# A two-layer SSM and MLP block, forward and backward: the main part taken chunk by chunk through both layers

## The chip, the cores and the metric

One core of a Trainium2 chip runs the kernel, in one launch. The time is device microseconds from the start to the end of an execution. PE is the matrix engine (its weight loads are listed apart, as PEld); DVE, ACT and POOL are the vector, scalar and GpSimd engines; SP issues DMAs only. PE sums into PSUM, which ACT and DVE empty; everything else lies in SBUF or, between distant stages, in device memory (names ending in `_d`).

## The reference

S = 2048 tokens, D = 448, F = 1792, one batch, bf16 outside and float32 in sums. `_A_ref` shifts k by a short convolution, multiplies by v, convolves with a long kernel by FFT and multiplies by q, which here is the normalised x; `_B_ref` is an MLP. Two layers use the same weights:

```python
def _B_ref(x, w1, w2):
    h = jnp.einsum("bsd,df->bsf", x, w1)
    h = _silu(h)
    return jnp.einsum("bsf,fd->bsd", h, w2)

x = A_q
x = x + _A_ref(_layernorm(x), A_k, A_v, A_shift_k, A_ssm_k, A_ssm_D)
x = x + _B_ref(_layernorm(x), B_w1, B_w2)
x = x + _A_ref(_layernorm(x), A_k, A_v, A_shift_k, A_ssm_k, A_ssm_D)
x = x + _B_ref(_layernorm(x), B_w1, B_w2)
```

Wanted are x and, for a given grad_out, the gradients of all eight inputs (A_q, A_k, A_v, A_shift_k, A_ssm_k, A_ssm_D, w1, w2). The convolution's result y is the same in both layers, since it doesn't depend on x: it is computed once, and its gradient is the sum of both layers' (`gY`).

## The kernel before

It has three parts. The **prefix** (0 to 109 us of the profile) computes y (`Ysb`) by FFTs as matmuls, stores the spectra, and normalises the first 512 tokens. The **main part** (`Main.run`, from 109.2 us) does the MLPs. The **suffix** (`_ssm_suffix`, first matmul at 563.6 us) takes the FFT back for the gradients of k, v, the kernels and D, and the rest of the weight gradients.

In the main part the tokens are four *chunks* of 512, each of four tiles of 128 tokens. X (float32, all 2048 tokens, in SBUF) holds the residual stream and later its gradient. For a chunk c and a layer L there are four products, each of 56 matmuls with 128x128 weights:

- **h** (L545): w1 by the transposed normalised x (`nT`), 14 blocks of F in banks of two (1024 columns of PSUM, two banks in turn). ACT takes silu from the bank (L549, `aT`), then DVE, or ACT once in a half, copies the same bank out (L551, `dT`), from which ACT later forms silu's slope (L532).
- **out** (L570): aT by w2, one tile of tokens per bank, added to X on DVE (L571). In layer 1, ACT copies X to bf16 and POOL stores it (L575, L577).
- **g** (L599): w2 transposed by the transposed gradient (`gT`); ACT copies (L603), DVE multiplies by the slope (L608, `ghT`).
- **n** (L640): ghT by w1 transposed; ACT scales (L642), DVE does the layer norm's backward (`ln_bwd`, four operations) and writes X; then the product with the first normalised x (`gyt`) and a second layer-norm backward, of the A half (L652).

The order is: layer 0 forward for chunks 0 to 3, layer 1 forward and backward for each chunk, layer 0 backward for chunks 0 to 3. Slopes' inputs, normalised rows and `gyt` of one layer are thus written to device memory and loaded again (`DT_d`, `N_d`, `GY_d`, in `load_l0`). The first half of the next h is issued before out of the present chunk. A scheduler fixes each engine's order by dependences and by estimated costs (`bal` shares copies between ACT and DVE); `high_priority` moves a step ahead.

The weight gradients sum over all 2048 tokens: per 128 of the 1792 rows ("ft"), 16 matmuls (L769) of `dstat` (activations with tokens on the partitions) by a tensor of rows. For them aT and ghT of each half chunk go to device memory: of layer 1 *turned*, by a transposing DMA on SP (L478) into one of two `turned` buffers and a store on POOL (L479); of layer 0 plain (L482), and then the load is a transposing DMA (L741). The w2 gradient is two sums: layer 0's from `mov2`, 10 fts beside layer 0 backward and 4 in the suffix, goes to `W2P_d` in float32 (L779) and is loaded and added later (L790, L795). The last thing is w1's gradient, 14 fts of 32 matmuls, each turned by PE and stored (L800 to L806).

In the suffix, L208 is the first FFT stage (its matrix `M1s` is loaded at L826), L228 and L229 the second inverse one, L879 and L880 its products, L916 the gradient of the long kernel (gK), L959 and L965 the gradient of k: DVE makes four products and PE sums them by matmuls with the identity.

Of the kernel before, what the change touches and what calls it, by code (L numbers as in the profile page):

```python
# [10 lines left out]
FP32 = mybir.dt.float32  # L11
# [6 lines left out]
P = 128  # L18
S = 2048
# [101 lines left out]
def kernel(  # L121
# [35 lines left out]
    k.N_d = [dram.tile([S, D], BF16, name=f"N_d{i}") for i in range(4)]  # L157
    k.DT_d = dram.tile([4, 2, P, NF // 2, 512], BF16, name="DT_d")
    k.A_d = [dram.tile([NF, P, S], BF16, name="A_d0"), dram.tile([P, NF, NT, P], BF16, name="A_d1")]
    k.GH_d = [dram.tile([NF, P, S], BF16, name="GH_d0"), dram.tile([P, NF, NT, P], BF16, name="GH_d1")]  # L160
    k.GY_d = dram.tile([S, D], BF16, name="GY_d")
    k.W2P_d = dram.tile([F, D], FP32, name="W2P_d")
# [18 lines left out]
    k.wk = ctx.enter_context(tc.tile_pool(name="wk", bufs=1))  # L181
    k.dp = ctx.enter_context(tc.tile_pool(name="dp", bufs=1))
    with tc.tile_pool(name="yk", bufs=1, side="right") as yk:
        k.Ysb = yk.tile([P, J, D], BF16, name="Ysb")
        _ssm_prefix(k)
        k.w1sb = k.wk.tile([DC, ND, F], BF16, name="w1sb", tag="WA")
        nc.sync.dma_start(out=k.w1sb[:], in_=k.B_w1.rearrange("(c p) f -> p c f", p=DC))
        k.w2sb = k.wk.tile([P, NF, D], BF16, name="w2sb", tag="WB")
        nc.sync.dma_start(out=k.w2sb[:], in_=k.B_w2.rearrange("(c p) d -> p c d", p=P))
        k.psum = ctx.enter_context(tc.tile_pool(name="psum", bufs=1, space=PSUM, reuse_waits="tile"))  # L190
        k.bal.reset()
        with ExitStack() as es:
            m = Main(k, es)
            m.run()
            with tc.issue_after(k.d0_load.ins):
                _wgrad_w2_first(k, m.td, range(10))
    _ssm_suffix(k)


# [36 lines left out]

def _swap_halves_dma(k, dst, src, lo, hi, eng, dlo=None):
    if dlo is None:
        dlo = lo
    dhi = dlo + (hi - lo)  # L240
    eng.dma_start(out=dst[0:64, dlo:dhi], in_=src[64:128, lo:hi])
    return eng.dma_start(out=dst[64:128, dlo:dhi], in_=src[0:64, lo:hi])
# [6 lines left out]
def _ln(k, pool, c, src, si, n_g, groups=((0, 4),), pin=False, eng=None):  # L249
    nc = k.nc  # L250
    for lo, hi in groups:
# [14 lines left out]
        k.bal.add("dve", 0.8 * n + 0.2)  # L266
        for tl in range(lo, hi):
            e = eng or k.bal.pick(D, act_ns=1.04, dve_ns=0.55, act_fixed=0.28)
            if e is nc.scalar:
                nc.scalar.activation(n_g[:, tl, :], src(tl), ACT.Identity, bias=nmr[:, tl:tl + 1], scale=r[:, tl:tl + 1])  # L270
            else:
                nc.vector.tensor_scalar(out=n_g[:, tl, :], in0=src(tl), scalar1=r[:, tl:tl + 1], scalar2=nmr[:, tl:tl + 1], op0=ALU.mult, op1=ALU.add)
    nc.gpsimd.dma_start(out=_pm(k.N_d[si][:])[:, 4 * c:4 * c + 4, :], in_=n_g[:])


def _ssm_prefix(k):
# [4 lines left out]
    with ExitStack() as es:  # L281
# [6 lines left out]
        k.M1sb = k.wk.tile([P, 16, 2, P], BF16, name="M1sb", tag="WA")  # L288
# [9 lines left out]
        ksb += [k.dp.tile([DC, S], BF16, name="K_sb", tag="dstat", bufs=2)[:] for i in range(2)]  # L298
# [116 lines left out]
        k.x0c0 = k.dp.tile([P, 4, D], BF16, name="x0c0", tag="dstat", bufs=2)  # L415
        nc.gpsimd.dma_start(out=k.x0c0[:], in_=_pm(k.A_q[0])[:, 0:4, :])
        k.na0 = k.dp.tile([P, 4, D], BF16, name="na0", tag="dstat", bufs=2)
# [40 lines left out]

class Main:

    def __init__(self, k, es):
# [3 lines left out]
        self.wt = pool("mwt")  # L465
        self.w2T = self.wt.tile([P, ND, F], BF16, name="w2T")
        self.w1T = self.wt.tile([P, NF, D], BF16, name="w1T")
        self.td = pool("mtd")
        self.ch = pool("mch")
        self.xp = pool("mx", side="right")  # L470
        self.X = self.xp.tile([P, NT, D], FP32, name="X")
        self.w1sb, self.w2sb, self.Y = k.w1sb, k.w2sb, k.Ysb

    def store_turned(self, dst, tile_, c, hh):
        nc = self.nc
        an = self.td.tile([P, NF // 2, 4, P], BF16, name="turned", tag="S", bufs=2)
        for lo, hi in ((0, 4), (4, 7)):
            nc.sync.dma_start_transpose(out=an[:, lo:hi].rearrange("p a t f -> p (a t) f"), in_=tile_[:, lo:hi, :].rearrange("p a s -> p (a s)"))  # L478
        nc.gpsimd.dma_start(out=dst[:, 7 * hh:7 * hh + 7, 4 * c:4 * c + 4, :], in_=an[:])  # L479

    def store_plain(self, dst, tile_, c, hh):
        self.nc.gpsimd.dma_start(out=dst[7 * hh:7 * hh + 7, :, 512 * c:512 * (c + 1)].rearrange("ft f s -> f ft s"), in_=tile_[:])  # L482

    def load_weights_T(self, which):
        nc, k = self.nc, self.k
        if which == 1:
            nc.sync.dma_start_transpose(out=self.w1T[:], in_=k.B_w1)
            return
        nc.sync.dma_start_transpose(out=self.w2T[:, 0:3, :], in_=k.B_w2[:, 0:384])
        nc.sync.dma_start_transpose(out=self.w2T[:, 3:4, :], in_=k.B_w2[:, 320:448])  # L490
        nc.gpsimd.memset(self.w2T[0:64, 3, :], 0.0)

    def transp(self, src, dst, blocks):
        nc, k = self.nc, self.k
        rows = max(hi - lo for lo, hi in blocks)
        for h in range(2):
            pt = k.psum.tile([P, 2, 512], BF16, name="ps_t", tag="tr", bufs=2)
            for u in range(2):
                lo, hi = blocks[2 * h + u]
                for tl in range(4):  # L500
                    nc.tensor.transpose(pt[:rows, u, tl * P:(tl + 1) * P], src[:, tl, lo:hi], k.ident[:])
            _copy(nc, k.bal.pick(1024, dve_ns=0.53), dst[:rows, 2 * h:2 * h + 2, :], pt[:rows])

    def a_fwd(self, c, si, xc, n_g=None, groups=((0, 4),)):
        nc, k, X = self.nc, self.k, self.X
        if n_g is None:
            n_g = self.ch.tile([P, 4, D], BF16, name="na", tag="na", bufs=2)
            src = (lambda tl: xc[:, tl, :]) if xc is not None else (lambda tl: X[:, 4 * c + tl, :])
            _ln(k, self.ch, c, src, si, n_g)
        t1 = self.ch.tile([P, 4, D], BF16, name="a_t1", tag="a_t1")  # L510
        for lo, hi in groups:
            sl = slice(4 * c + lo, 4 * c + hi)
            nc.vector.tensor_tensor(out=t1[:, lo:hi, :], in0=n_g[:, lo:hi, :], in1=self.Y[:, sl, :], op=ALU.mult)
            nc.vector.tensor_tensor(out=X[:, sl, :], in0=xc[:, lo:hi, :] if xc is not None else X[:, sl, :], in1=t1[:, lo:hi, :], op=ALU.add)
        k.bal.add("dve", 3.1)
        return n_g

    def b_pre(self, c, si, groups=((0, 4),), eng=None):
        X = self.X
        n_g = self.ch.tile([P, 4, D], BF16, name="nb", tag="nb", bufs=2)  # L520
        _ln(self.k, self.ch, c, lambda tl: X[:, 4 * c + tl, :], si, n_g, groups, eng=eng)
        return n_g

    def b_tr(self, n_g):
        nT = self.ch.tile([P, ND, 512], BF16, name="nT", tag="nT", bufs=2)
        self.transp(n_g, nT, [(DC * i, DC * i + DC) for i in range(4)])
        return nT

    def slope(self, d):
        for o in range(0, 7, 2):  # L530
            n = min(2, 7 - o)
            self.nc.scalar.activation(d[:, o:o + n, :], d[:, o:o + n, :], ACT.Derivative_silu)  # L532
        self.k.bal.add("act", 3.4)

    def h(self, c, L, nT, half, hold):
        nc, k = self.nc, self.k
        aT = self.td.tile([P, NF // 2, 512], BF16, name="aT", tag="T", bufs=3)
        dT = self.td.tile([P, NF // 2, 512], BF16, name="dT", tag="D", bufs=3)
        hold.append((aT, dT))
        for ft0, n in ((0, 2), (2, 2), (4, 2), (6, 1)) if half == 0 else ((7, 1), (8, 2), (10, 2), (12, 2)):  # L540
            ps = k.psum.tile([P, 2, 512], FP32, name="ps_h", tag="mm", bufs=2)
            for u in range(n):
                ft = ft0 + u
                for dc in range(ND):
                    nc.tensor.matmul(ps[:, u, :], lhsT=self.w1sb[:, dc, ft * P:(ft + 1) * P], rhs=nT[:DC, dc, :], start=(dc == 0), stop=(dc == ND - 1))  # L545
            o = ft0 - 7 * half
            a = aT[:, o:o + n, :]
            tm = dT[:, o:o + n, :]
            nc.scalar.activation(a, ps[:, 0:n, :], ACT.Silu)  # L549
            e = nc.scalar if o == 4 else nc.vector  # L550
            _copy(nc, e, tm, ps[:, 0:n, :])  # L551
            k.bal.add("act", 0.52 * n)
            k.bal.add(*(("act", 0.52 * n) if e is nc.scalar else ("dve", 0.6 * n)))
        if L == 1:
            if half == 1:
                for _, d in hold:
                    self.slope(d)
        else:
            nc.gpsimd.dma_start(out=k.DT_d[c, half], in_=dT[:])
            self.store_plain(k.A_d[0], aT, c, half)  # L560
        if L == 1:
            self.store_turned(k.A_d[1], aT, c, half)

    def out(self, c, aT, last):
# [435 lines left out]
```

## Time and profile before

| | |
|---|---|
| median of 3 timed runs | 848.54 us (840.52 to 859.15) |
| span of the profiled execution | 867.0 us |
| mean clock granted to PE in it | 0.950 |
| instructions | 12590 |
| PE, DVE, ACT busy | 753.6, 527.9, 478.0 us |
| DMA: packets, data | 168391, 178.59 MB |
| prefix, main part, suffix | 0–109.2, 109.2–563.6, 563.6–867.0 us |

The span runs from the first to the last instruction of one execution, taken by the profiler; the timed runs are others. PE's ends are modelled, so its busy time is an upper reading. The page's groups give busy time, mean duration, and the idle time just before an instruction with what ended it: idle time of an engine that nobody waits for costs nothing. The costliest groups of PE, and the DMA that most rows below refer to (issue to landing):

```profile
L599 PE MATMUL ps_g<-gT,w2T 128*128 128x512 bf16 x431 | 104.7, 388 | 17.3 <-ACT ghp L603 16.3
L545 PE MATMUL ps_h<-nT,w1sb 112*128 112x512 bf16 x448 | 106.5, 385 | 3.1 <-ACT nT L111 1.9
...
L113 DVE CAST dT<-ps_h 128x1024 bf16<-128x1024 f32 (+1 forms) x56 | 59.2, 1065 | 31.7 <-ACT aT L549 31.6
```
```profile
A_d<-turned POOLq DMA_DIRECT2D x8, 896.0 KB, 4.7
GH_d<-turned POOLq DMA_DIRECT2D x8, 896.0 KB, 7.3
dTl<-DT_d SPq DMA_DIRECT2D x8, 896.0 KB, 6.0
...
dstat<-A_d SPq DMA_DIRECT2D x14, 512.0 KB, 6.6
dstat<-GH_d SPq DMA_DIRECT2D x14, 512.0 KB, 3.8
```

### The profile page before, as it was taken

The numbers are of one execution on the slowest core, as the hardware profiler recorded it, in microseconds if no ns is written. First come the engines' busy times: TensorE is split into PE (matmuls) and PEld (weight loads), VectorE is DVE, ScalarE is ACT, GpSimd is POOL, SyncE is SP. The second block draws the span as 40 slices with busy tenths as digits, with TensorE's granted clock in tenths as the row PEclk, the third lists the DMA queues.
The fourth block names the chain that finished last, engine by engine and source line by source line (L and its number), as shares of the span: only waits on it lengthen the run. The fifth ranks groups of instructions, "written<-read, shape, count | busy, mean of one in ns | idle before, by whom it ended". The sixth has DMA issues, their size and how long they took to land.

```text
span 867.0 us, 12590 instructions
## 1 busy us (share of the span) xinstructions
PE 753.6 (87%) x4894; PEld 411.7 (47%) x4924; DVE 527.9 (61%) x1060; ACT 478.0 (55%) x573; POOL 143.0 (16%) x218
## 2 busy tenths in 40 slices
PE   6998699999999999999779899950579996999997
PEld 4975344444444444444334344520346664545553
DVE  5789668777349788682779899730156631760100
ACT  5789566669879798998566552230136532330010
POOL 1143223221100211101001011110101121221010
PEclk9999789999999999999899999985789998999999
DMA  9279896656586677899774656999988879987771
GB/s 333 91 244 283 301 248 239 230 211 170 142 173 157 188 196 196 197 210 247 181 251 153 187 170 164 266 177 137 186 260 300 284 258 254 130 236 175 185 186 44
DMA packets 168391, 178.59 MB, mean 206 GB/s; under 512 B 135374, under 2 KB 139086, under 8 KB 167308
## 3 DMA queue, kind: packets, MB, share of 16 engines
q1 hardware_dynamic: 144304, 81.70, 42.0%
q0 software_dynamic: 21696, 88.07, 31.7%
q10 hardware_dynamic: 2332, 8.03, 3.1%
q8 instruction: 38, 0.62, 0.3%
q14 instruction: 21, 0.17, 0.1%
HBM read 66.64 MB, written 70.65 MB: 158 GB/s over the span
## 4 chain that ended last, share of the span: by engine, by line
DVE 18%; DMA 18%; issue 17%; PE 16%; ACT 10%; POOL 2%; POOLq 0%; ACTq 0%; SPq 0%; DVEq 0%
DMA dstat<-A_d 6%; PE ps_d L769 6%; PE ps_o L570 3%; DVE dT L113 3%; DVE lb_u L624 2%; DVE X L625 2%; DMA dTl<-DT_d 2%; ACT ghp L603 2%; DVE lb_junk L621 2%; PE ps_h L545 2%; DMA out_dram<-gKD 2%; PE ps_n L640 2%; DVE ghT L608 2%; DMA dmov<-in_grad_out_dram 2%; DMA xsw_c<-Zg 1%
## 5 line engine op out<-in xcount | busy, mean ns | idle before, releaser
L769 PEld LDWEIGHTS <-dstat 128*128 128x128 bf16 x896 | 87.7, 99 | 122.5 <-DMA dstat<-A_d 39.9
L769 PE MATMUL ps_d<-mov,dstat 128*128 128x448 bf16 x448 | 96.1, 358 | 39.0 <-DMA dstat<-A_d 39.0
L599 PE MATMUL ps_g<-gT,w2T 128*128 128x512 bf16 x431 | 104.7, 388 | 17.3 <-ACT ghp L603 16.3
L545 PE MATMUL ps_h<-nT,w1sb 112*128 112x512 bf16 x448 | 106.5, 385 | 3.1 <-ACT nT L111 1.9
L769 PE MATMUL ps_d<-dmov,dstat 128*128 128x448 bf16 x448 | 97.1, 360 | 4.6 <-DMA dmov<-N_d 2.2
L640 PE MATMUL ps_n<-w1T,ghT 128*128 128x448 bf16 x448 | 93.4, 360 | 4.6 <-ACT lb_u L642 3.5
L570 PE MATMUL ps_o<-w2sb,aT 128*128 128x448 bf16 x448 | 91.5, 353 | 0.8 <-ACT aT L549 0.3
L113 DVE CAST dT<-ps_h 128x1024 bf16<-128x1024 f32 (+1 forms) x56 | 59.2, 1065 | 31.7 <-ACT aT L549 31.6
L599 PEld LDWEIGHTS <-w2T 128*128 128x128 bf16 x448 | 44.4, 99 | 71.6 <-issue 24.9
L603 ACT CAST ghp<-ps_g 128x1024 bf16<-128x1024 f32 x56 | 56.6, 1010 | 34.8 <-PE ps_g L599 12.7
L549 ACT ACTIVATE aT<-ps_h 128x1024 bf16<-128x1024 f32 (+1 forms) x64 | 58.1, 917 | 27.1 <-PE ps_h L545 15.9
L545 PEld LDWEIGHTS <-w1sb 112*128 112x128 bf16 x448 | 44.1, 99 | 57.7 <-issue 12.7
L640 PEld LDWEIGHTS <-ghT 128*128 128x128 bf16 x448 | 43.6, 99 | 49.8 <-issue 9.4
L570 PEld LDWEIGHTS <-aT 128*128 128x128 bf16 x448 | 42.9, 98 | 43.7 <-ACT aT L549 3.8
L800 DVE CAST dout<-ps_d 128x448 bf16<-128x448 f32 x14 | 8.7, 624 | 75.6 <-PE ps_d L769 75.6
L805 ACT COPY do<-ps_dt 112x512 bf16<-112x512 bf16 x14 | 8.2, 586 | 75.1 <-PE ps_dt L803 75.1
L228 PE MATMUL ps_v<-Gsb,pa 128*128 128x128 bf16 x336 | 43.5, 221 | 6.5 <-DVE pa L437 4.1
L229 PE MATMUL ps_v<-Gsb,pb 128*128 128x128 bf16 x336 | 42.0, 222 | 3.1 <-DVE pb L438 1.5
L532 ACT ACTIVATE dTl<-dTl 128x1024 bf16<-128x1024 bf16 (+1 forms) x32 | 28.7, 947 | 18.2 <-DMA dTl<-DT_d 18.2
L608 DVE TENSOR_TENSOR ghT<-dT,ghp 128x1024 bf16<-128x1024 bf16 (+1 forms) x32 | 19.6, 622 | 31.0 <-ACT ghp L603 31.0
L229 PEld LDWEIGHTS <-pb 128*128 128x128 bf16 x336 | 32.7, 99 | 11.9 <-DVE pb L438 5.2
L113 DVE COPY Zg<-ps_tr 128x2048 bf16<-128x2048 bf16 x5 | 6.0, 1222 | 51.0 <-DMA W2P_d<-dpo 47.4
(182 smaller groups left out, 1300.1 us busy)
## 6 DMA issues: line engine op xcount, KB each, us to landing
A_d<-aT POOLq DMA_DIRECT2D x8, 896.0 KB, 5.0
DT_d<-dT POOLq DMA_DIRECT2D x8, 896.0 KB, 6.3
A_d<-turned POOLq DMA_DIRECT2D x8, 896.0 KB, 4.7
GH_d<-turned POOLq DMA_DIRECT2D x8, 896.0 KB, 7.3
dTl<-DT_d SPq DMA_DIRECT2D x8, 896.0 KB, 6.0
GH_d<-ghT POOLq DMA_DIRECT2D x8, 896.0 KB, 8.4
dstat<-A_d SPq DMA_DIRECT2D x14, 512.0 KB, 6.6
dstat<-GH_d SPq DMA_DIRECT2D x14, 512.0 KB, 3.8
```

What stands on the lines that cost most here:

```text
L113: eng.tensor_copy(out, in_)
L228: nc.tensor.matmul(pv[:, i, :], lhsT=pa[:, i * P:(i + 1) * P], rhs=k.Gsb[:, ga, :], start=True, stop=False)
L229: nc.tensor.matmul(pv[:, i, :], lhsT=pb[:, i * P:(i + 1) * P], rhs=k.Gsb[:, gb, :], start=False, stop=True)
L532: self.nc.scalar.activation(d[:, o:o + n, :], d[:, o:o + n, :], ACT.Derivative_silu)
L545: nc.tensor.matmul(ps[:, u, :], lhsT=self.w1sb[:, dc, ft * P:(ft + 1) * P], rhs=nT[:DC, dc, :], start=(dc == 0), stop=(dc == ND - 1))
L549: nc.scalar.activation(a, ps[:, 0:n, :], ACT.Silu)
L570: nc.tensor.matmul(po[:, :D], lhsT=aT[ft // 7][0][:, ft % 7, tl * P:(tl + 1) * P], rhs=self.w2sb[:, ft, :], start=(ft == 0), stop=(ft == N ...
L599: nc.tensor.matmul(ps[:, u, :], lhsT=self.w2T[:, b, ft * P:(ft + 1) * P], rhs=gT[:, b, :], start=(b == 0), stop=(b == ND - 1))
L603: nc.scalar.copy(gh[:], ps[:])
L608: nc.vector.tensor_tensor(out=ghT[hh][:, o:o + len(u), :], in0=dT[hh][1][:, o:o + len(u), :], in1=gh[:, u[0]:u[0] + len(u), :], op=ALU.mult)
L640: nc.tensor.matmul(pn[:, :D], lhsT=ghT[ft // 7][:, ft % 7, tl * P:(tl + 1) * P], rhs=self.w1T[:, ft, :], start=(ft == 0), stop=(ft == NF - 1))
L769: nc.tensor.matmul(ps[:, :D], lhsT=st[:, t, :], rhs=movs[gi][:, t, :], start=(gi == 0 and t == 0), stop=(gi == len(groups) - 1 and t == NT ...
```

## The change

The main part goes chunk by chunk: a chunk's layer 1 backward is followed at once by its layer 0 backward, and the next chunk's forward is laid between. PE's order in the main part and the suffix is the order of the program text (`manual_schedule`), no longer the scheduler's; the other engines are still scheduled.

```diff
+    with tc.manual_schedule(engines={nc.tensor.engine}):
         with ExitStack() as es:
-            m = Main(k, es)
-            m.run()
-            with tc.issue_after(k.d0_load.ins):
-                _wgrad_w2_first(k, m.td, range(10))
-    _ssm_suffix(k)
+            Main(k, es).run()
+        _ssm_suffix(k)
```

Per chunk (jobs are steps of four matmuls of the weight gradients):

```diff
+            gh = self.G(gT, hook=mid_g)
+            aT, dT = self.H(c, 1, nT, range(7))
+            self.slope(dT)
+            if c < 3:
+                self.fwd0(c + 1)
+            self.O(c, 1, aT)
+            self.scale(gh, dT)
+            for hh in range(2):
+                self.store(("g", 1), gh[hh], c, hh)
...
+            self.N(c, 1, gh, lambda tl: gb[:, tl, :], self.n1[1], self.n1[0], hook=mid_n)
...
+            if c < 3:
+                aT, dT1 = self.H(c + 1, 0, nT, (1, 4), hook=mid_h)
+                gb = gb_load(c + 1)
+            else:
+                jobs.start()
+                jobs.run(14)
...
+            gh = self.G(gT, dT0)
...
+                self.slope(dT0)
+                self.O(c + 1, 0, aT, hook=None)
+                self.fwd1(c + 1)
...
+            self.N(c, 0, gh, lambda tl: self.X[:, 4 * c + tl, :], self.n0[c][1], self.n0[c][0], hook=mid_n1)
```

So g of layer 1 comes before h of that layer and is scaled by the slope afterwards (`scale`). X is bf16. `DT_d`, `GY_d` and `W2P_d` are gone; `Y_d` and `G1_d` (y, and the gradient after the layer 0 MLP) are new. aT of both layers is stored turned, in quarter chunks (the two `turned` buffers hold four blocks each):

```diff
-        an = self.td.tile([P, NF // 2, 4, P], BF16, name="turned", tag="S", bufs=2)
         for lo, hi in ((0, 4), (4, 7)):
+            an = self.t([P, 4, 4, P], "turned", "S", 2)
...
+            nc.gpsimd.dma_start(out=dst[:, 7 * hh + lo:7 * hh + hi, 4 * c:4 * c + 4, :], in_=an[:, 0:hi - lo])
```

In layer 1 the output is stored from X itself, which the following n overwrites; the layer norm's backward has five operations:

```diff
-            ob = self.ch.tile([P, 4, D], BF16, name="ob", tag="a_t1")
-            nc.scalar.copy(ob[:], X[:, 4 * c:4 * c + 4, :])
-            nc.gpsimd.dma_start(out=_pm(k.outs[0][0])[:, 4 * c:4 * c + 4, :], in_=ob[:])
+        if L == 1:
+            nc.gpsimd.dma_start(out=_pm(k.outs[0][0])[:, 4 * c:4 * c + 4, :], in_=X[:, 4 * c:4 * c + 4, :])
...
+    nc.vector.scalar_tensor_tensor(out=v[:], in0=u0, scalar=-1.0 / D, in1=n_t, op0=ALU.mult, op1=ALU.mult, accum_out=cp[:, 1:2])
+    nc.vector.tensor_scalar(out=cc[:], in0=cp[:, 0:1], scalar1=-1.0 / D, scalar2=None, op0=ALU.mult)
+    nc.vector.tensor_scalar(out=v[:], in0=n_t, scalar1=cp[:, 1:2], scalar2=cc[:], op0=ALU.mult, op1=ALU.add)
+    nc.vector.tensor_tensor(out=v[:], in0=v[:], in1=u0, op=ALU.add)
+    nc.vector.tensor_tensor(out=G_out, in0=v[:], in1=g_res, op=ALU.add)
```

Normalising is done on DVE alone. In h, silu and the copy alternate per bank (in layer 1 all copies on DVE, in layer 0 those of two banks). All four weight layouts are loaded after the prefix, in the pool `mwt`. The matrix M1s is loaded to space that `mwt` had.

Each ft of w2's gradient is one sum of 32 matmuls (grad_out by a of layer 1, then X, which holds the gradient between the layers, by a of layer 0), and those of w1 as before; all are `Jobs`, of which 24 steps run in the last chunk, and one or two after each step of the suffix, the rest at its end:

```diff
+        keys = (("a", 1), ("a", 0))
+        yield from self.pair((0, 1), keys, (go, g2), self.fin_w2, 12)
...
+        keys = (("g", 1), ("g", 0))
+        yield from self.pair((0, 1), keys, (mov3, mov1), self.fin_w1, NT)
```

In the suffix, swapped halves of the spectrum are DVE copies, no longer DMAs; k's gradient is summed on DVE (64 products of 128x448 and 48 additions for 32 products of 128x896 and 64 matmuls); and the layer-norm backward of the first A half, with its 16 tiles, is done there after loads of `G1_d`, `N_d` and `Y_d`:

```diff
+            for j in range(4):
+                nc.vector.tensor_tensor(out=prods[j], in0=gks[:, g + j, :], in1=skb[:, j, :], op=ALU.mult)
+            for j in range(2):
+                nc.vector.tensor_tensor(out=s_[j][:], in0=prods[2 * j], in1=prods[2 * j + 1], op=ALU.add)
...
+            nc.vector.tensor_tensor(out=gk[:, g % 2, :], in0=s_[0][:], in1=s_[1][:], op=ALU.add)
...
+            nc.vector.scalar_tensor_tensor(out=u1, in0=G1, scalar=k.rstd[0][:, t:t + 1], in1=y, op0=ALU.mult, op1=ALU.mult, accum_out=cp[:, t % 4, 0:1])
+            _ln_bwd(k, p2, u1, n0, cp[:, t % 4, :], G1, G1)
```

## The prediction

> **What bounds the kernel now.** I read the page's busy shares first, by engine and in 40 slices of 21.7 us, with the clock that PE was granted.
>
> ```profile
> ## 1 busy us (share of the span) xinstructions
> PE 753.6 (87%) x4894; PEld 411.7 (47%) x4924; DVE 527.9 (61%) x1060; ACT 478.0 (55%) x573; POOL 143.0 (16%) x218
> ## 2 busy tenths in 40 slices
> PE   6998699999999999999779899950579996999997
> PEld 4975344444444444444334344520346664545553
> DVE  5789668777349788682779899730156631760100
> ACT  5789566669879798998566552230136532330010
> ...
> PEclk9999789999999999999899999985789998999999
> ```
>
> PE is the bound nearly everywhere. It falls at the start, in slices 20 and 21 (layer 0 backward), and to 5, 0 and 5 in slices 27 to 29. What stops it is in the table of waits (waiting engine, tile and line; what it waits for; us in all, times, longest), then in the timeline of SP (start, duration):
>
> ```profile
> POOL GH_d L479 <- DMA turned<-ghT: 67.6, 8, 11.2
> ...
> PE ps_d L769 <- DMA dstat<-A_d: 39.0, 2, 38.3
> ...
> ACT dTl L532 <- DMA dTl<-DT_d: 18.2, 6, 6.7
> ...
> PE ps_g L599 <- ACT ghp L603: 16.3, 9, 5.6
> ```
> ```profile
> 560.73 53.73 SPq L741 DMA_TRANSPOSE dstat<-A_d  x3
> ```
>
> One wait of 38.3 us on PE is for transposing loads of A_d[0], which hold SP's queue for 53.7 us. The busy time by windows (length, then busy us of PE, weight loads, DVE, ACT and POOL, then PE's clock, the DMA share, GB/s) shows the hole, and the thinner stretch of layer 0 backward, where slopes come back from DT_d:
>
> ```profile
> 440.00:460.00 20.00, 15.11 (x67) 7.00 (x68) 14.22 (x33) 11.47 (x17) 0.23 (x1) 0.91 0.45 161
> ...
> 480.00:500.00 20.00, 15.29 (x77) 7.26 (x78) 15.52 (x36) 13.42 (x19) 0.93 (x1) 0.91 0.51 157
> ...
> 580.00:600.00 20.00, 0.00 (x0) 0.00 (x0) 0.00 (x0) 0.00 (x0) 0.00 (x0) 0.50 1.00 125
> 600.00:620.00 20.00, 5.13 (x15) 2.14 (x16) 0.00 (x0) 0.91 (x1) 1.07 (x2) 0.51 1.14 106
> ```
>
> The profiled span is 867.0 us, 18.5 above the median of 848.5 and above the slowest timed run (859.2). I take the hole to be what varies (some 20 us in a median run). The change removes it, so the sum against the profile needs no further shift to be a median.
>
> **The change, part by part.** *PE's work.* A 512-column matmul follows the one before by 0.213 us, one of 448 columns by 0.188, one of 128 by 0.055. Each of h, g, out and n has 56 matmuls per chunk and layer: 11.9 us for h or g (512 columns), 10.5 for out or n (448). Over both layers that is 4 × 11.9 + 4 × 10.5 = 89.8, and 64 transposes of 0.055 add 3.6: 93.4 us per chunk, 373.5 for four, before and after. Before, the main part lasts from 109.2 to 563.6; less 160 matmuls of L769 (30 us) that is 424, so 51 us were waits and slow clock. Moved: 24 steps of four L788 matmuls (18 us) now stand in the last chunk, so the suffix gets 64 more of them than before (+12), and loses 64 gk matmuls of L965 (−12).
>
> *Removed.* The 38.3 us hole and the slow clock after it (660 − 615 = 45 us at 0.87: about 4): −42. A_d[0] is now stored turned, so its loads in the w2 sum are plain, as `dstat<-GH_d` is (3.8 us to landing). What is late next there is M1s (below). The write and reload of slopes, GY_d and W2P_d go (18.2, 3.9 and 47.4 us of waits on ACT and DVE); the last is inside the hole, and PE feels only the 16.3 us at L599 of the others.
>
> *Added at the start.* w1, w2T, w2 and w1T load only when the prefix has freed its space (w1 before: during the prefix). Nearest rows: a load of 896 KB lands in 6.0 us; at best it is covered by chunk 0's LN, at worst all 9 show: I take 3. The first grad_out load stands behind w1T's transpose on SP: 0 to 9, I take 6. Chunk 0's third LN has no n matmuls beside it (9), and the first layer-1 h waits for DVE, which has chunk 1's two LNs first (6). Sum 24.
>
> *Added per chunk, c = 0 to 2.* PE's order is now fixed: what comes late can't be passed over. Three stalls.
> (a) out0 is stored straight from X (L600), where before ACT copied it (L575). The first write of n(c, layer 1) into X, last operation of the layer-norm backward on DVE, must wait for that store to land. On POOL it stands behind four turned pieces of a and two of g, each waiting for its SP transpose and for one of two `turned` buffers. The row for such waits is POOL L479, 67.6 us in 8: 8.5 each. From out's end: the first scaling about 1; then two transposes and two stores, 8.5 by that row; out0's own issue and landing 5 (896 KB land in 4.7 to 7.3 in the table of DMA issues): 14.5. The first X write could go 2.6 (14 matmuls) + 0.6 (L642) + 2 (four operations) after PE begins n, which waits for the four scalings (about 4): 9. So DVE stands some 5 us, up to 13 where the pieces of a are still queued, and nothing at best; I take 7. Behind it in DVE's queue: all of n's layer-norm work, the gT copy, and the `dT` copies of the next h (L574's bank is free only then); ACT can't start the next u0, with three buffers. DVE doesn't catch up: a tile of n in layer 1 is two backwards of 0.62 + 0.08 + 0.17 + 0.35 + 2 × 0.39, then 0.39 and 0.76 = 5.2 us (0.39 from 0.62 at 896 and 1.09 at 1792 elements), against PE's 2.6. Two tiles of work are thus left when PE is done, and the stand on top: PE waits at the second to fifth bank of h for 7.9 + 3.8 + 1.9 + 0.6 = 14. If the store lands first, about 5 of these remain.
> (b) Both copies of a bank in series: silu 1.02, dT copy 1.22 (before also: 31.6 us in all of DVE's waits for silu) is 2.24 for a bank while two banks give PE 3.4; nearly covered, 0.4 per bank at the ends of h: 2.
> (c) h's tail to g: gT's ACT copy 1.0 and a table load 1.28 stand before g: 2.2; h of layer 1 waits for g's last copies and its first silu for a table: 1.3 + 2.5.
> I take 20 a period (bounds 8 and 26), three periods: 60.
>
> One operation has no row: `tensor_scalar` of 128x448 bf16. Nearest below, 112x112 bf16 takes 0.247; above, 128x448 from f32 takes 0.503. I take 0.35; there are 28 a period, so the ends are ±0.10 to 0.15 × 28 = 3 to 4 us of DVE a period, or ±10 in all. The Trainium skill ("VectorE: DVE Perf Modes", the perf-mode tier table) lets a bf16 tensor_scalar from SBUF run four results per cycle, and by its figures I estimate 0.18 for it; the whole would then be about 14 us shorter, and no row of this trace decides it.
>
> *The clock.* 440–460 and 480–500 were granted 0.91 after waits of up to 5.6 us: 1.8 us each. A stand of 7.9 per period costs the same again; 6 in all, within the bounds above. The Trainium skill ("TensorE: Matmul & The Clock Gate", Part 1: The HAM clock gate) halves the clock after an idle window of about 3.4 us; by this the fixed order pays only where one stall is long, and would pay nothing for (b) and (c).
>
> *Last chunk to stage 1.* go's load starts when w2's space is free, after the last out: 4.4. One more X write by DVE before gT can be turned: 9. M1s (1 MB, 8.1 us to landing at L826, which high priority put early) now lies over w1T, so it waits for the last n matmul, behind G1_d's stores on POOL: 13. Sum 27, bounds 12 to 32.
>
> *Suffix.* Before: 303.4, of it 42 the hole. PE's other waits after 615 are 5.7 + 3.7 + 7.7 + 7.5 = 25 (span less busy in the windows 615–660, 660–700, 700–754, 754–867). Jobs woven into each step cover about 5 of them; gK's stage stays without cover (15, before 8 to 15). The tail: gk's sums go from PE to DVE: 64 × 0.39 + 48 × 0.39 to 0.62 = 43 to 55 us, and the third layer-norm backward comes from the main part: 16 × (0.76 + 0.70 + 0.17 + 0.35 + 0.78) = 44. In DVE's order 13 of the 16 gk groups stand between the third and the fourth `dout` copy (L847) of w1's gradient, and PE can go two fts further (6.45 each) on its banks. So 13 × 2.7 to 3.4 = 35 to 44, less 13: 22 to 31, and smaller ones between out1's tiles, 2 to 12. I take 30. Suffix: 303 − 42 − 5 + 30 = 286.
>
> Sum: 109 + 373.5 + 18 + 24 + 60 + 27 = 611.5, + 286 = 897.5.
>
> **Rivals.** *A, PE flows.* The price is (a)'s stall. out0 lands before n's first X write if a turned piece makes its round in under 4 us. For: `A_d<-turned` lands in 4.7 for twice the bytes, and traffic falls (slopes 7.3 MB written and read, W2P_d 3.2 and 3.2, of 137 in all). Against: POOL's 8.5 us per wait. With it a period costs 8 (−36), and with the cheap tensor_scalar (−10) and a tail of 20 (−10) the time is 842; with the start and the turn at their low ends (−10 and −15) it is 817, the side of faster. It decides at a round of 4 us. *B, in between:* out0 late by 3 us, periods of 14, tail 20: 870. *C, transposes jam again:* 48 turned transposes in the main part for 32, each issued by the one SP queue, and 14 transposing loads of g in the tail. A single stretch like the 53.7 us on SP adds 35: 933. Against it: they are spread over 500 us, and none of the 32 of before shows such a time. That the change does not do what it says is no rival here: in the listing of the changed program each w2 tile is one sum of 32 matmuls, and PE has the emitted order.
>
> **How the numbers follow.** The forecast, 0.51: 898, its own range 872 to 920. A: 0.24 (817 to 850, more of it in the lower half). B: 0.13 (850 to 872). C: 0.12 (920 to 945). To leave out no more than 2 in 10 the range runs from 830 (0.13 of A below) to 930 (half of C above). A measurement of this kernel tells 2% from none: faster is under 831.6, slower over 865.5. Slower: the forecast, C and half of B, 0.70. Within: the other half of B and 0.09 of A, 0.15. Faster: the rest of A, 0.15.
>
> **What would show it.** In the changed profile: DVE's X at n of layer 1 waiting for `out_dram<-X`, with out0's store (L600) landing after PE's first n tile; PE's idle at ps_h of the next chunk's layer 0; stage 1 waiting for M1s; no DMA wait at the plain loads of a; PE idle in the tail for `dout`, with DVE at nine tenths. It is wrong if PE shows nines from 130 to 540, or DVE has under six tenths in the last 100 us.

## The result, and the profile after

The changed kernel takes 944.12 us (median of 4, 939.31 to 945.81) where the kernel before took 853.85 on the same chip: a ratio of 1.116, with a 95% interval of 1.108 to 1.124. Some runs of the kernel before are in a slower state of the clock: its median has them, the ratio leaves them out. It is slower, as forecast, but the forecast of 898 is 46 us short and the time lies outside the range. The profiled span is 937.5 us at a mean clock of 0.920.

The page's busy shares, in 40 slices of 23.4 us:

```profile
## 1 busy us (share of the span) xinstructions
PE 750.4 (80%) x4831; PEld 413.5 (44%) x4860; DVE 541.9 (58%) x1275; ACT 388.9 (41%) x460; POOL 155.6 (17%) x247
## 2 busy tenths in 40 slices
PE   6987478796898968979689994949999982954867
PEld 4965233352443524534245442425666651522433
DVE  4789315748387474875738446343655410998560
ACT  4788355444624447255471640213555530200000
...
PEclk9999779899999979999799997979999987886989
```

The hole of before (5, 0, 5) is gone, and with it every long wait for A_d. In its place PE has a six at slices 10, 15 and 20, one for each of three periods, with a lowered clock (7) at the last two; then there are two dips around the last chunk (slices 25 and 27), one at slice 34, and one at 36 and 37, where DVE has a nine and an eight. The waits name them (engine, tile and line; what it waits for; us in all, times, longest):

```profile
DVE X L748 <- DMA out_dram<-X: 30.9, 4, 12.6
...
PE ps_dt L860 <- DVE dout L847: 35.6, 5, 23.1
PE ps_gkv L985 <- ACT A1g L987: 20.7, 1, 20.7
PE ps_h L571 <- DVE dT L113: 19.9, 21, 3.4
PE ps_h L571 <- DVE nT L113: 18.7, 5, 4.8
PE ps_s L205 <- DMA M1s<-c_m: 13.2, 1, 13.2
...
PE ps_d L788 <- DMA turned<-ghT: 11.4, 1, 11.4
```

Set beside the prediction's sum, from the starts of the stages on PE (h of layer 1 of chunk 0 at 171.4, of chunk 3 at 526.3, stage 1 at 633.5; what is above PE's matmuls is waits and slow clock):

| part | PE's matmuls | waits, predicted | waits, measured |
|---|---|---|---|
| 109.2 to 171.4, the start | 37.0 | 24 | 25 |
| 171.4 to 526.3, three periods | 280.2 | 60 | 75 |
| 526.3 to 633.5, last chunk to stage 1 | 74.2 | 27 | 33 |
| suffix, as a whole | – | 286 | 304 |

That is 22 us too little in the main part and 18 in the suffix; the median lies 6.6 above the profiled span, which the sum left out.

One period at its worst place, in the timeline (start, duration, instruction, and in brackets the idle time before it with what ended it):

```profile
203.52 0.78 POOL L497 DMA_DIRECT2D g_d<-turned  x1 [5.79 <-DMA turned<-ghT]
206.73 0.74 POOL L497 DMA_DIRECT2D g_d<-turned  x1 [2.42 <-DMA turned<-ghT]
207.46 0.58 POOL L600 DMA_DIRECT2D out_dram<-X  x1
...
212.07 0.39 DVE L748 TENSOR_TENSOR X<-lb_v,gb 128x448 bf16<-128x448 bf16 x1 [6.23 <-DMA out_dram<-X]
...
217.06 1.44 PE L571 MATMUL ps_h<-nT,w1sb 112*128 112x512 bf16 x3 [4.81 <-DVE nT L113]
```

POOL stands for two of the turned pieces of g, only then issues out0's store; DVE stands 6.23 us for that store before its first write to X; and PE, done with n at 211.8, waits for DVE to reach the copy of nT. This is the chain of part (a) of the prediction.

### The profile page after: what moved, and what is told of

It is laid out like the page before. It is cut to its first block, busy times and chain, and to the rows that moved or that the text cites. A ratio compares the mean times of both kernels' runs of the same rounds, so it can differ in the third digit from the quotient of the medians.

```text
span 937.5 us, 12449 instructions
## 1 busy us (share of the span) xinstructions
PE 750.4 (80%) x4831; PEld 413.5 (44%) x4860; DVE 541.9 (58%) x1275; ACT 388.9 (41%) x460; POOL 155.6 (17%) x247
## 4 chain that ended last, share of the span: by engine, by line
PE 30%; DVE 23%; issue 16%; DMA 15%; ACT 10%; POOL 5%; SPq 0%; POOLq 0%; DVEq 0%; ACTq 0%
PE ps_d L788 8%; PE ps_h L571 6%; PE ps_o L594 5%; ACT dT L587 3%; DMA turned<-ghT 3%; DMA out_dram<-gK 3%; DVE dT L113 2%; DMA out_dram<-X 2%; POOL rstd L265 2%; PE ps_g L610 2%; DVE A1g L1012 2%; ACT aT L574 2%; DVE lb_v L743 2%; DVE n L272 2%; DVE ln_st L258 2%
## 5 line engine op out<-in xcount | busy, mean ns | idle before, releaser
L571 PE MATMUL ps_h<-nT,w1sb 112*128 112x512 bf16 x448 | 120.5, 428 | 47.3 <-DVE dT L113 19.9
L610 PE MATMUL ps_g<-nT,w2T 128*128 128x512 bf16 x432 | 101.7, 382 | 12.0 <-ACT nT L111 7.6
L643 ACT ACTIVATE lb_u<-ps_n,rstd 128x448 bf16<-128x448 f32 x32 | 20.3, 633 | 138.9 <-PE ps_n L641 75.1
L617 ACT CAST ghT<-ps_g 128x1024 bf16<-128x1024 f32 (+1 forms) x48 | 44.4, 939 | 43.0 <-PE ps_g L610 43.0
L788 PE MATMUL ps_d<-go,dstat 128*128 128x448 bf16 x224 | 52.1, 370 | 11.5 <-DMA turned<-ghT 11.4
L587 ACT ACTIVATE dT<-dT 128x1024 bf16<-128x1024 bf16 (+1 forms) x48 | 53.8, 1189 | 0.1
L497 POOL DMA_DIRECT2D a_d<-turned x32 | 24.4, 761 | 170.3 <-DMA turned<-aT 153.8
L788 PE MATMUL ps_d<-n3m,dstat 128*128 128x448 bf16 x224 | 50.8, 379 | 0.0
L788 PE MATMUL ps_d<-X,dstat 128*128 128x448 bf16 x224 | 48.9, 353 | 1.8 <-DMA dstat<-a_d 1.6
L788 PE MATMUL ps_d<-n1m,dstat 128*128 128x448 bf16 x224 | 47.1, 357 | 0.0
```

Source lines behind the costliest of these rows:

```text
L497: nc.gpsimd.dma_start(out=dst[:, 7 * hh + lo:7 * hh + hi, 4 * c:4 * c + 4, :], in_=an[:, 0:hi - lo])
L587: self.nc.scalar.activation(dT[hh][:, o:o + n, :], dT[hh][:, o:o + n, :], ACT.Derivative_silu)
L610: nc.tensor.matmul(ps[:, u, :], lhsT=self.w2T[:, b, ft * P:(ft + 1) * P], rhs=gT[:, b, :], start=(b == 0), stop=(b == ND - 1))
L617: nc.scalar.copy(g, ps[:, lo:hi, :])
L788: self.nc.tensor.matmul(ps[:, :D], lhsT=st[:, t, :], rhs=mov[:, t, :], start=(first and t == 0), stop=(last and t == NT - 1))
```

## The experiments

Times are medians of timed executions. The runs were made in four groups, and ratios are to the kernel before in the same group (839.9, 841.9, 840.9 and 838.8 us, medians of the runs that the ratios use).

**The late store of out0.**

```diff
-            nc.gpsimd.dma_start(out=_pm(k.outs[0][0])[:, 4 * c:4 * c + 4, :], in_=X[:, 4 * c:4 * c + 4, :])
+            for lo in (0, 2):
+                ob = self.t([P, 2, D], "ob", "pr", 3)
+                sl = slice(4 * c + lo, 4 * c + lo + 2)
+                nc.scalar.copy(ob[:], X[:, sl, :])
+                nc.gpsimd.dma_start(out=_pm(k.outs[0][0])[:, sl, :], in_=ob[:])
```

> Undoes one part: out of layer 1 is copied by ACT to a buffer of its own (two halves of 128x896) and stored from there, as before the change, so that no write to X waits for a store. Theory 1 (the late store of out0 sets the periods): the 30.9 us of DVE waits for out_dram<-X go to nothing, PE's waits at h of the next chunk fall by 8 to 14 us in each of three periods, and the time falls by 25 to 40, to 904 to 919 us. Rival (the layer norm's backward on DVE, 5.2 us a tile against PE's 2.6, sets the period with or without the store): DVE's wait goes, but the copies of h still come behind the same work, and the time falls by less than 12 us.

914.9 us, ratio 1.090 (1.083 to 1.097), against 1.110 to 1.116 of the changed kernel. DVE's wait for the store is gone, and the three periods (from the first n of layer 1 to the fourth) take 333 us for 351 (355 in the second profile of the changed kernel): the stand costs 6 to 7 us in each. At the last chunk PE's wait before the job steps is 5.9 us, now for the load of grad_out, where it was 11.4: there n's last tiles hold the banks that the job steps need, until ACT finds space that DVE frees. (The first profile and two others name a DMA for that wait; in the profiles of five other runs it is ACT's L643, with 10.8 to 11.1 us.) Together some 24 us. Theory 1 holds in its cause: the time is in the range that it gave, 21 to 29 us less, but a period gains 6 to 7 us where it said 8 to 14, and PE's waits at h for `dT` stay (22.3 us).

**PE's order.** The line that fixes it is taken out; the program, the work of every engine and the bytes are the same. The order of the other engines is not: the scheduler makes it anew.

```diff
-    with tc.manual_schedule(engines={nc.tensor.engine}):
+    if True:
```

> The changed kernel itself, on the chip of the three runs beside it, as what they are compared with. Both theories: 935 to 948 us, with the waits of its first profile (30 us of DVE for out_dram<-X, 20 us at ps_gkv, 35 us at ps_dt, 13 us for M1s).

> PE's order is left to the scheduler again in the main part and the suffix; nothing else is changed. Theory 1 (the waits are of data and space, which any order meets; the fixed order costs only where a stand could be passed over with jobs): within 15 us of the changed kernel, 925 to 955. Rival (the fixed order is itself the loss, as nothing may pass a late step): 30 us or more faster, under 912.

936.0 us for the changed kernel, 898.4 with the scheduler's order, ratios 1.110 and 1.066. My theory 1 fell: this edit alone is worth 38 us, and stage 1 begins 41 us earlier (592.6 for 633.5). One window over the main part of each, of the changed kernel first, then with the scheduler's order (length; busy us of PE, weight loads, DVE, ACT, POOL; clock, DMA share, GB/s):

```profile
110.00:630.00 520.00, 428.71 (x2125) 206.15 (x2141) 301.14 (x746) 230.34 (x280) 72.32 (x99) 0.92 0.58 146
```
```profile
110.00:590.00 480.00, 420.54 (x2124) 202.13 (x2139) 301.96 (x747) 230.36 (x280) 73.79 (x101) 0.94 0.64 160
```

The same number of matmuls and the same 230 us of ACT and 301 of DVE fit into 480 us instead of 520. No engine is short of time in either. In the fixed order PE stands because its next instruction isn't ready, and may take no other.

That is not all of the 38 us, for POOL's order changed with PE's. With the scheduler's order POOL issues out0's store before the turned pieces of g, where it stood behind two of them (207.46 in the timeline above):

```profile
197.60 0.58 POOL L600 DMA_DIRECT2D out_dram<-X  x1 [1.18 <-DVE X L596]
204.48 0.39 DVE L748 TENSOR_TENSOR X<-lb_v,gb 128x448 bf16<-128x448 bf16 x1 [3.09 <-DMA out_dram<-X]
205.15 0.75 POOL L497 DMA_DIRECT2D g_d<-turned  x1 [6.97 <-DMA turned<-ghT]
```

DVE's four waits for that store are 9.9 us in all, for 30.9. So part of what this edit gains is the store's stand again. No run gave POOL and DVE their new order with PE's fixed, so the shares are not known.

**What h waits for, in the fixed order.** Two edits: each half of a bank emptied by itself, and no copy of layer 0's h on DVE.

```diff
-            for lo, hi in self.parts(fp):
+            for lo, hi in ((0, 1), (1, 2)):
```
```diff
-                aT, dT1 = self.H(c + 1, 0, nT, (1, 4), hook=mid_h)
+                aT, dT1 = self.H(c + 1, 0, nT, (), hook=mid_h)
```

> In h each half of a bank (512 columns) has its own silu and its own copy, in place of one of each for the pair; the matmuls and their order are as they are. Theory 2 (what is left of a period without the store of out0, 111 us against 93.4 of matmuls, is mostly h itself: silu and copy of a bank in series take 2.2 us and two banks give PE 3.4 only if they start in time; slow clock comes with these short stands): after the last matmul of a bank 1.3 us of emptying are left for 2.2, each of the eight h gets 1.5 to 3 us shorter, and the time falls by 12 to 25 us. Rival (h waits because DVE's queue holds the layer norms' work before the copies): DVE gets 1 us more work per h, and the time stays within 5 us or rises.

> The changed kernel with its fixed PE order, but ACT makes all copies of layer 0's h (chunks 1 to 3), DVE none. Theory 2a (in the fixed order these two copies stand in DVE's queue behind n's layer-norm backward, and PE can't go round them): h of layer 0 gets 3 to 6 us shorter each, the time falls by 8 to 20 us. Rival (ACT then has silu and copy for every bank, 2.0 us against PE's 1.7, and becomes the bound of this h): within 6 us of the changed kernel.

The first gave 963.1 us, 27 more than the changed kernel of its group; the second 928.9, ratio 1.101 (1.090 to 1.111) against 1.110 (1.096 to 1.124). In the first, a silu now often waits for DVE's copy, I take it of the other half of the same pair of banks, as the group of silus shows (busy, mean ns; idle before, with what ended it):

```profile
L574 ACT ACTIVATE aT<-ps_h 128x512 bf16<-128x512 f32 x112 | 66.4, 603 | 70.6 <-PE ps_h L571 38.8 <-DVE dT L113 31.5
```

In the changed kernel of that group the full-size silus have 46.5 us of idle time, of which 46.1 are for PE. So theory 2 as I put it fell: finer steps give DVE's lateness one more place to enter. Whether a shorter emptying would help without that isn't shown, as the edit brought the new wait with it. In the second run layer 0's h is shorter, 17.6 us each for 19.6 to 21.1; PE's waits between the banks of the first one fall from 4.5 us (2.19, 1.94 and 0.41) to 1.4, though ACT alone now empties a bank in 2.0 us. This speaks for the rival of the first run, that h waits for DVE's queue. The 7 us between the medians agree with three such gains, but the intervals overlap. In neither run does h come near its 11.9 us of matmuls; in the second most of what is left is slow clock (0.85 from 214.8 to 232.4).

**The tail.**

```diff
-        self.nc.vector.tensor_copy(o[:], ps[:, :D])
+        self.nc.scalar.copy(o[:], ps[:, :D])
```

> The copy of each finished w1 sum out of PSUM goes from DVE to ACT, which is nearly idle there. Theory 1 (those copies stand in DVE's queue behind the sums of k's gradient and the third layer-norm backward): PE's waits at ps_dt (35.6 us) go, and the time falls by 20 to 35 us, to 909 to 924. Rival (DVE's own work of about 90 us after 800 us ends last): PE ends earlier, but the last instruction is DVE's or its store, and less than 12 us are gained.

914.1 us, ratio 1.087 (1.079 to 1.096): 22 to 30 us less, and the waits at ps_dt are gone. One window of the tail, of the changed kernel and of this one (columns as above):

```profile
840.00:860.00 20.00, 3.71 (x13) 1.83 (x14) 20.00 (x57) 0.58 (x1) 4.42 (x8) 0.50 0.20 62
```
```profile
840.00:860.00 20.00, 20.00 (x116) 10.75 (x114) 19.63 (x58) 3.06 (x6) 6.53 (x11) 1.00 0.92 252
```

DVE is full in both; PE goes from 3.7 to 20. The copies of 0.62 us each were late only because they stood behind other work in DVE's queue. At the end the third layer-norm backward on DVE (to 899 us of 906) and the last stores of w1's gradient now finish together; more was gained than the rival's 12 us.

**The wait at ps_gkv.** Around 760 to 800 us the changed kernel shows this:

```profile
775.17 21.44 SPq L782 DMA_TRANSPOSE dstat<-g_d  x1
776.85 0.54 POOL L1027 DMA_DIRECT2D A1g<-N_d  x1 [3.05 <-DMA out_dram<-gK]
795.60 0.69 DVE L1030 SCALAR_TENSOR_TENSOR A1g<-A1g,rstd 128x448 bf16<-128x448 bf16 x1 [22.11 <-DMA A1g<-G_d]
...
798.18 0.91 ACT L987 CAST A1g<-ps_gkv 128x896 bf16<-128x896 f32 x1 [22.86 <-DVE A1g L1012]
```

The first product of the third layer-norm backward stands in DVE's queue for its load; the products that free gkv's space are behind it; ACT and then PE wait. Meanwhile one transposing load holds SP for 21.4 us. Two edits: L1030 ordered after k's gradient; and those loads made plain (w1's gradient is then another quantity).

```diff
+            with tc.issue_after(gk_i.ins):
+                nc.vector.scalar_tensor_tensor(out=u1, in0=G1, scalar=k.rstd[0][:, t:t + 1], ...
```
```diff
-            nc.sync.dma_start_transpose(out=st[:], in_=src[ft, :, :])
+            nc.sync.dma_start(out=st[:], in_=src[ft, :, :].rearrange("p (t q) -> p t q", q=P))
```

> Only the order in the suffix: the products L1030 that begin the third layer-norm backward come after the last sum of k's gradient on DVE, instead of one standing in front of the products that free gkv's space. Theory 1: PE's one wait of 20.7 us at ps_gkv goes, since DVE no longer stands 22.1 us for the load of G1_d; 18 to 22 us less, 922 to 926 us. Rival (the loads are late for everything there, and whatever comes first waits): less than 8 us gained, and another wait for a load of 15 us or more appears in the window 765 to 800.

> The loads of the layer-0 g operand for w1's gradient are plain instead of transposing, of the same bytes (w1's gradient is then another quantity). Theory 1 (the transposing loads, two of 15.2 and 21.4 us on SP around 755 to 797 us, hold up all other DMAs): the waits for G1_d (39.8 us in all on DVE) and for gK's store fall below 10, and the time falls by 20 to 30 us, to 914 to 924. Rival (the loads of the third layer-norm backward are late because POOL issues them behind stores that wait): the waits for G1_d stay above 25 us, and the time moves by less than 8 us.

935.7 us (924.4 to 943.2; ratio 1.109) and 928.3 (ratio 1.106, 1.095 to 1.117): neither is clear of the changed kernel. In the first the wait at ps_gkv goes, and two others take its place:

```profile
PE ps_dt L860 <- DVE dout L847: 47.2, 5, 36.9
...
DVE A1g L1016 <- DMA out_dram<-A1g: 27.5, 1, 27.5
```

In the second ps_gkv's wait is 13.9 us for 20.7. Both theories 1 fell, and the numbers are those of the rivals: 0 and 8 us between the medians, other waits in place of the first, and 26.6 us of waits for G1_d left in the second. The order on DVE only chooses who waits, and the transposing loads are at most a third of that wait (without any such edit it was 18.1 us in the second profile of the changed kernel, and 13.2 in the run on M1s below). The second rival's reason, a late issue by POOL, is not what the trace shows: the loads of G1_d are issued at 766.9 and 770.9 and take 19.7 us to land. The loads of v, k and KS_d, gK's stores and these loads are on their way together between 755 and 800 us; that this is why they are slow is likely but not shown, for from 784 to 790 the DMA engines were only 0.38 busy. Which of them would have to move wasn't tried.

**M1s.**

```diff
+        jobs.run(18)
         for n2 in range(16):
```

> 18 steps of weight-gradient matmuls (13.5 us) are taken from the tail and run before the first FFT stage of the suffix, under the load of M1s; 18 fewer are left at the end. Theory 1 (PE's 13.2 us wait for M1s is bare): it falls under 2 us, and the time falls by 9 to 14 us. Rival (the work that is moved is missing later, where the tail waits for DVE's copies): the wait at ps_dt grows by as much, and the time stays within 4 us.

928.1 us, ratio 1.105 (1.088 to 1.122): 8 us between the medians, not clear of nothing. M1s is no longer waited for, but PE waits 10.8 us there for a load of `dstat` instead, and 9.3 at gK where it was 4.3:

```profile
PE ps_d L788 <- DMA dstat<-a_d: 12.3, 3, 10.8
...
PE ps_gK L967 <- ACT gK L111: 9.3, 2, 7.8
```

**Putting them together.** Scheduler's order and ACT's copies; then also out0 from its copy; then also the third layer-norm backward in the main part:

```diff
             else:
+                u1 = self.t([P, D], "lb_u1", "lb_u0", 3)
+                nc.vector.scalar_tensor_tensor(out=u1[:], in0=Gt, scalar=k.rstd[0][:, t:t + 1], in1=self.Y[:, t, :], ...
...
+                _ln_bwd(k, self.ch, u1[:], n_a[:, tl, :], cp[:, 4 + tl, :], Gt, Gt)
                 if tl % 2:
-                    nc.gpsimd.dma_start(out=_pm(k.G1_d[:])[:, t - 1:t + 1, :], in_=g1[:])
+                    nc.gpsimd.dma_start(out=_pm(k.outs[1][0])[:, t - 1:t + 1, :], in_=g1[:])
```

> Two edits that were tried alone are put together: PE's order by the scheduler (alone 898, where the changed kernel had 936) and the copies of w1's finished sums on ACT (alone 914). Theory 3 (the two losses lie apart, one in the main part, one in the tail, and add up): the wait at ps_dt, 61.6 us with the scheduler's order, goes, and the time is 850 to 875. Rival (the tail ends with DVE's own work, about 90 us after 760): 880 to 895.

> As the run before it in this list, and out of layer 1 stored from a copy (alone 915, 20 us or so under the changed kernel). Theory 3: under the scheduler's order PE passes over the late n and takes other matmuls, so that the late store costs less than in the fixed order: 0 to 10 us less than the run without it. Rival (the store is late for DVE in either order, and DVE is the next bound): 15 us or more less.

> As the run before it in this list, and the third layer-norm backward is done in the main part at each tile of n of layer 0, as before the change, with no stores and loads of G1_d and Y_d. Theory 3 (in the tail these 44 us of DVE end last and wait for their loads; in the main part DVE has room): 20 to 40 us less than the run without it, 820 to 850, PE over nine tenths in the last 100 us. Rival (DVE is then the bound of the main part): the main part gets 20 us longer or more, and the time is the same within 10 us.

860.4, 852.7 and 826.7 us, ratios 1.017 (1.005 to 1.029), 1.011 (1.004 to 1.017) and 0.978 (0.967 to 0.989). The first two together give 76 us, more than the 38 and 22 that they gave alone: they are not independent, as with the scheduler's order alone the wait at ps_dt had grown from 36 to 61.6 us. Out0's copy, worth over 20 in the fixed order, is worth 8 between the medians here (the intervals overlap). The number is theory 3's, the reason only in part: the stand for the store had itself shrunk, to 7.9 us in four waits before the copy. The third step gives 26.

Then the fixed order was put back into that version, and, in another run, 12 job steps with early space before stage 1:

```diff
-        k.dp3 = jobs.dp3 = pool("dp3")
+        k.dp3 = pool("dp3")
+        jobs.run(12)
+        jobs.dp3 = k.dp3
```

> The fastest kernel so far (out0 from a copy, w1's finished sums copied by ACT, the third layer-norm backward in the main part, the scheduler's PE order: 827) with the fixed PE order put back. Theory A (the fixed order costs by itself, about 40 us, since h's banks are emptied slower than PE fills them and nothing may go between): 860 to 885. Theory B (it costs only by the late steps that the other edits took away, of which out0's store is the largest): 830 to 850.

> The fastest kernel so far, with 12 steps of weight-gradient matmuls, loaded to space that is free early, before the first FFT stage of the suffix. If PE's 16.5 us wait there is for space of the main part that the loads need, 8 to 14 us less, 813 to 820; if it is for the transfers themselves, within 4 us of it.

864.9 us, ratio 1.029 (1.020 to 1.038), and 816.2, ratio 0.971 (0.964 to 0.978). Theory A's number holds: without these three late steps, the store of out0 above all, the fixed order still costs 38 us (other late steps stay: PE waits 22.0 us for M1s there). It does so before stage 1 of the suffix, which begins at 620.3 us with the fixed order and at 580.7 with the scheduler's. Where in it, the groups of h and g on PE show, with the fixed order and then with the scheduler's:

```profile
L570 PE MATMUL ps_h<-nT,w1sb 112*128 112x512 bf16 x448 | 112.3, 404 | 34.5 <-DVE dT L113 25.7 <-ACT dT L111 6.5 <-ACT nT L111 2.3
L613 PE MATMUL ps_g<-nT,w2T 128*128 128x512 bf16 x432 | 106.2, 398 | 11.8 <-ACT nT L111 6.8 <-DVE nT L113 3.4 <-ACT ghT L620 0.4
```
```profile
L570 PE MATMUL ps_h<-nT,w1sb 112*128 112x512 bf16 x448 | 106.3, 386 | 7.4 <-DVE dT L113 5.7 <-ACT nT L111 0.6 <-DVE nT L113 0.2
L613 PE MATMUL ps_g<-nT,w2T 128*128 128x512 bf16 x448 | 102.6, 384 | 2.6 <-DVE nT L113 1.5 <-ACT ghT L620 0.7
```

Idle time before h falls from 34.5 to 7.4 and before g from 11.8 to 2.6: 36 us, of which 7 come back at the transposes (ps_t). One h of layer 1 shows two causes, first with the fixed order, then with the scheduler's:

```profile
281.67 1.15 DVE L258 BATCH_NORM_STATS2 ln_st<-X 128x6 f32<-128x448 bf16 x2
...
283.33 2.34 DVE L113 CAST dT<-ps_h 128x1024 bf16<-128x1024 f32 x2
284.59 8.11 PE L570 MATMUL ps_h<-nT,w1sb 112*128 112x512 bf16 x24 [5.28 <-DVE dT L113]
```
```profile
263.44 0.93 PE L593 MATMUL ps_o<-w2sb,aT 128*128 128x448 bf16 x4
...
265.09 2.35 DVE L113 CAST dT<-ps_h 128x1024 bf16<-128x1024 f32 x2
266.37 3.61 PE L570 MATMUL ps_h<-nT,w1sb 112*128 112x512 bf16 x16 [1.05 <-DVE dT L113]
...
267.36 1.15 DVE L258 BATCH_NORM_STATS2 ln_st<-X 128x6 f32<-128x448 bf16 x2
```

With the scheduler's order PE lays matmuls of out between the banks of h. But DVE's order differs too: the copies out of h's banks stand before the statistics of the next layer norm, where with the fixed order three of these come first. So the 38 us are the price of fixing PE's order together with the order that the scheduler then gave DVE; the two were not taken apart.

The last run beats both kernels, by 3% the one before. Its expectation for space holds: PE's longest wait for `dstat` there, 16.5 us, is 5.8 now, and the time fell by 10.5.

## Why the prediction was short

The direction and the places were right, four of them with their sizes: DVE's stand for out0 (7 predicted, 6.0 to 6.2 in the three periods), M1s (13 and 13.2), the tail behind DVE's queue (30 and 35.6, and removing it gave 22 to 30), and the start (24 and 25). The hole of A_d went, as predicted.

The step that failed is (b), with what was made of (a). I let h's banks be "nearly covered", 2 us a period, and put the loss at h (14) on out0's stand, of which 5 were to be left without it. With (b) and (c) that is 13 us a period without the stand (rival A even had 8) and 22 with it, of which the sum took 20. Measured are 25 with the stand and 18 without it: the stand costs 6 to 7 where I had 9, and the rest 18 where I had 13. Without the stand a period is still 109 to 113 us for 93.4 of matmuls. In the changed kernel's profile h of layer 0 takes 20 us (217 to 237) and h of layer 1 16 (291 to 308) for 11.9 each. What the runs show in place of "nearly covered" is that a bank is emptied late because the copy is in DVE's queue behind layer-norm work: with these copies on ACT, PE's waits inside the first such h fell from 4.5 to 1.4 us. In a fixed order PE has nothing else to do meanwhile. I named that DVE doesn't catch up, and priced it only together with the store. How the 38 us of the last comparison divide between PE's order and DVE's stays open.

The clock was mis-sized: I had 6 us for it and left them inside the bounds, so the sum has none. h's matmuls alone took 120.5 us where before they took 106.5, 14 us more, and the windows from 280 to 360 us were granted 0.91, 1.00, 0.83 and 0.91. By the rule of the Trainium skill ("TensorE: Matmul & The Clock Gate", Part 1: The HAM clock gate), a halved clock after an idle window of about 3.4 us, I took (b) and (c) to be spared. The trace shows slow matmuls after shorter stands than that; 16 of them take 3.6 us at full clock:

```profile
291.39 5.31 PE L571 MATMUL ps_h<-nT,w1sb 112*128 112x512 bf16 x16 [2.98 <-DVE nT L113]
297.31 3.64 PE L571 MATMUL ps_h<-nT,w1sb 112*128 112x512 bf16 x16 [0.61 <-DVE dT L113]
...
345.78 7.03 PE L571 MATMUL ps_h<-nT,w1sb 112*128 112x512 bf16 x24 [1.94 <-DVE dT L113]
```

In the suffix, 18 us were missing. The wait at ps_gkv (20.7) was in no term; rival C, a jam around transposing loads, had 35 us for something like it and a chance of 0.12. It is no jam of transposes alone (at most a third by the plain loads): a load that took long to land, with a place at the head of DVE's queue. gK's stage, which I charged with 15, waited 4.3.

In the last chunk I had 9 us for gT's turn and 4.4 for go's load. The turn was covered by the 14 job steps, and these themselves began 11.4 us late. I put that down to out0's stand (12.6 us there), which kept n's banks: the same cause, one place earlier. With the copy of out0 the wait is 5.9 us.

The operation without a row, tensor_scalar of 128x448 bf16, took 0.39 us (0.35 taken; the 0.18 estimated from the page is far off). Rivals A and B needed out0's store in time; where that was given, in the run with the copy, the time was still 915, with 18 us a period, so their 8 and 14 were not reached in this fixed order.

## What to carry to other kernels

When an order of instructions is fixed, price each producer's queue, not only its duration: a step that is emptied by an engine with other work in its queue stands as long as that work, and PE has nothing to do meanwhile. Look at the other engines' order as well: here an edit of PE's order alone moved a store on POOL and copies on DVE. Before a large rewrite is judged, take its parts apart: here a chunk-by-chunk version with one sum for w2 came out 2% faster than the kernel before (0.978), while the fixed order, a store from a live buffer, a copy on the wrong engine and a step put off to the tail had taken it from 827 to 936 us, with shares that depend on one another. A freed wait can show up again at the next one, as those at ps_gkv and for M1s did here; the time, not the wait, tells what was gained.

## What the runs showed of the hardware

A bf16 tensor_scalar with two per-partition scalars runs no faster than a tensor_tensor of the same shape. Groups of DVE in the changed kernel (busy, mean ns):

```profile
L746 DVE TENSOR_SCALAR lb_v<-n,cp,lb_cc 128x448 bf16<-128x448 bf16 x48 | 18.9, 394 | 0.7
L747 DVE TENSOR_TENSOR lb_v<-lb_v,lb_u 128x448 bf16<-128x448 bf16 x48 | 18.7, 390 | 0.6
```

The Trainium skill ("VectorE: DVE Perf Modes", the perf-mode tier table) gives the first operation twice the rate of the second; these rows differ from it. A plain copy does have the higher rate here: 64x2048 bf16 took 0.69 us (L235), where products of 128x1024 took as long (L926).

The time that one transposing load of 512 KB holds SP varies widely, in one and the same profile too: in the 827 us version 2.2 us at 690.5 and 14.2 at 700.1 (share of the DMA engines 0.86 and 1.01), and 21.4 at 775.2 in the changed kernel. What sets it isn't shown: in the last case the DMA engines had a share of 1.09 from 780 to 800 us and moved 111 GB/s, but from 784 to 790 only 0.38 and 27 GB/s.
